# A decode block on Trainium2: the first weight load issued as two on the same queue, 16 partitions and then the other 112

## The chip, the cores and the metric

The kernel runs on one core of a Trainium2 chip. The metric is the time of one execution on the device in microseconds (us), as the median of several runs. Everything is float32. The five engines named below are TensorE (PE in the profile, with PEld for its loads of stationary operands), VectorE (DVE), ScalarE (ACT), GpSimd (POOL) and SyncE (SP). DMAs are issued from SP or from ACT, each of which has a queue of its own, and the DMA engines carry them out.

## What is computed

One decode step of a transformer block for eight sequences with one new token each: layer norm, attention over the last 1024 positions of a cache, then layer norm and a gated feed-forward layer, both with a residual.

```python
B, D = 8, 1024;  Hq, Hkv, Dh = 32, 4, 128;  Df = 3584
def _A_ref(x, k_cache, v_cache, wq, wo):
    W = min(4096, max(256, Sk // 4))                 # 1024
    q = (x @ wq).reshape(B, 1, Hq, Dh).transpose(0, 2, 1, 3)
    k = repeat(k_cache[:, :, Sk - W:, :], Hq // Hkv, axis=1)
    v = repeat(v_cache[:, :, Sk - W:, :], Hq // Hkv, axis=1)
    p = softmax(einsum("bhqd,bhkd->bhqk", q, k) * Dh ** -0.5)
    o = einsum("bhqk,bhkd->bhqd", p, v)
    return o.transpose(0, 2, 1, 3).reshape(B, 1, Hq * Dh) @ wo
def _B_ref(x, w_gate, w_up, w_down):
    return (gelu(x @ w_gate) * (x @ w_up)) @ w_down
h  = x + _A_ref(layernorm(x), k_cache, v_cache, wq, wo)
h2 = h + _B_ref(layernorm(h), w_gate, w_up, w_down)      # the result
```

## The kernel before

With eight rows of activations, nearly all the work is bringing weights and cache from HBM into SBUF. These are laid out on the host into twelve units of 128 partitions by 16,384 floats (65,536 bytes for each partition, 8.39 MB for each unit): two for wq, two for the keys, two for the values, two for wo, and four for gate and up, the last two of which carry some rows of w_down besides. What is left of w_down follows as four loads `dn`, three `tails` and two `ends`, which get smaller towards the end of the kernel.

There are two buffers in SBUF, `wbuf[0]` and `wbuf[1]`, each as large as one unit. Even units go to the first and odd units to the second. All weight loads are issued by `move` (line 91) on SP's queue in one order, in the loop of lines 150 to 155: units 0 and 1 without a wait, and unit u from 2 on after the matmuls that read unit u - 2. Those waits hold up SP, so all later loads stand behind them. In the first turn of that loop, x (eight rows of 4,096 bytes, into partitions 0, 4, ..., 28 of `x_sb`) is issued on ACT's queue, behind a memset of `x_sb` on GpSimd.

A load adds 16 to a semaphore when all of it has landed. Units count on `go[0]` or `go[1]`, one for each buffer. VectorE adds 1 more to it when the stationary operands of that unit (`still[0]` or `still[1]`) are ready, and TensorE's `half` (line 214) takes 17 from it before it begins its 64 matmuls on the buffer. So a half begins when both its weights and its activations are there.

The steps up to the first matmuls on weights are: x lands; `layernorm` (line 247) on VectorE, with one square root on ScalarE, writes `source`; TensorE transposes it in eight pieces into `turned` (line 240); `spread(0)` (line 271) copies `turned` with VectorE into `still[0]` and `still[1]`, one copy for each, each adding its 1 to `go`; then `half(0, ...)` reads unit 0 and, in the next turn of TensorE's loop, `half(1, ...)` reads unit 1. `spread` is called again at the second layer norm, as `spread(5)`.

`run` (line 80) gives an instruction the waits it is handed: `start` (line 71) leaves out those that the engine has already seen, issues all but the last as waits of their own, and puts the last on the instruction.

Of the kernel before, what the change touches and what calls it, by code (L numbers as in the profile page):

```python
# [7 lines left out]
P = 128  # L8
# [6 lines left out]
NC = D // P  # L15
NQ = 4
# [25 lines left out]
class Flow:  # L42
# [37 lines left out]
    def run(self, engine, make, *waits, mark=True, gives=None):  # L80
        ins = self.start(engine, make, waits)
        if gives is not None:
            ins.then_inc(*gives)
            return None
        if not mark:
            return None
        self.done[engine] += 1
        ins.then_inc(self.own[engine], 1)
        return self.own[engine], self.done[engine]

    def move(self, name, out, src, *waits, engine="sync", sem=None):
        s = self.sem(name) if sem is None else sem
        self.start(engine, lambda e: e.dma_start(out, src), waits).then_inc(s, 16)  # L93
        return s, 16


def decode_block(nc, x, units, dn, tails, ends, outs):

    fl = Flow(nc)
    run, move = fl.run, fl.move  # L100
# [10 lines left out]
    wbuf = [space[:, i * BUF:(i + 1) * BUF] for i in range(2)]  # L111
# [6 lines left out]
    go = [fl.sem("go_a"), fl.sem("go_b")]  # L118
# [4 lines left out]
    at_mark = {}  # L123
# [26 lines left out]
    for u in range(UNITS):  # L150
        k, i = divmod(u, 2)
        free = None if k == 0 else (half_a, half_b)[i](k - 1)
        move(f"u{u}", wbuf[i], units[u], free, sem=go[i])
        if u == 0:
            x_in = move("x", x_sb[0:ROWS:STEP, :], x, x_zero, engine="scalar")

# [19 lines left out]
    for i, (n, src) in enumerate(zip(ENDS, ends)):  # L176
        t = wbuf[1][:, c0:c0 + NQ * n]
# [69 lines left out]
    def layernorm(src, ready, name, room):  # L247

        bn = sb(name + "_bn", ROWS, D // N, 6)
        tok = None  # L250
        for i in range(D // N):
            tok = run("vector", lambda e, i=i: e.bn_stats(bn[:, i], src[:, i * N:(i + 1) * N]), ready)
        mv, ve, sd, r0, r1, r2, rs = (
            sb(f"{name}_{n}", ROWS, k) for n, k in
            (("mv", 2), ("ve", 1), ("sd", 1), ("r0", 1), ("r1", 1), ("r2", 1), ("rs", 1))
        )
        tok = run("vector", lambda e: e.bn_aggr(mv, bn), tok)
        tok = run("vector", lambda e: e.tensor_scalar(ve, mv[:, 1:2], EPS, None, op0=ALU.add), tok)
        tok = run("scalar", lambda e: e.activation(sd, ve, AF.Sqrt), tok)
        tok = run("vector", lambda e: e.reciprocal(r0, sd), tok)  # L260

        tok = run("vector", lambda e: e.scalar_tensor_tensor(
            r1, r0, r0, ve, op0=ALU.mult, op1=ALU.mult), tok)
        tok = run("vector", lambda e: e.tensor_scalar(
            r2, r1, -0.5, 1.5, op0=ALU.mult, op1=ALU.add), tok)
        tok = run("vector", lambda e: e.tensor_mul(rs, r0, r2), tok)
        run("vector", lambda e: e.tensor_scalar(
            source[0:ROWS], src, mv[:, 0:1], rs, op0=ALU.subtract, op1=ALU.mult), tok, room,
            gives=(go_turn, 1))

    def spread(k):

        for i in range(2):
            run("vector", lambda e: e.tensor_copy(  # L274
                still[i].rearrange("p (c j m) -> p c j m", c=NC, j=NQ),
                turned.rearrange("p (c m) -> p c m", c=NC)[:, :, 0:32].unsqueeze(2).to_broadcast(
                    [P, NC, NQ, 32])), at_mark["t", k], gives=(go[i], 1))


    layernorm(x_sb, x_in, "ln1", src_ok)  # L280
    spread(0)


    side_by_side = [source[:, hf * N:(hf + 1) * N] for hf in range(2)]
# [12 lines left out]
    for hf in range(2):  # L297
# [3 lines left out]
        for s in range(2):  # L301
            for a in range(2):
                for b in range(HB):
# [6 lines left out]
                        gives=(go[hf], 1) if end else None)  # L310
# [3 lines left out]
    for hf in range(2):  # L314
# [7 lines left out]
        if hf == 1:  # L322
            run("vector", lambda e: e.tensor_copy(still[0], turned), at_mark["t", 2], half_a(1),
                gives=(go[0], 1))
# [4 lines left out]
        gives=(go[1], 1))  # L329


    for hf in range(2):
# [3 lines left out]
        for h in range(2):  # L336
            o3 = sums[hf][:, h * N:(h + 1) * N].rearrange("p (b d) -> p b d", b=HB)
            for b in range(HB):
# [5 lines left out]
                else:  # L344
# [3 lines left out]
                        gives=(go_turn, 1) if end and hf else None)  # L348
        cleared[hf] = run("gpsimd", lambda e: e.memset(still[hf], 0.0), done(2))  # L349

    for hf in range(2):
# [12 lines left out]
        gives=(go_fold, 1))  # L364
    h_sb = sb("h_sb", ROWS, D)
    h_ok = run("vector", lambda e: e.tensor_add(h_sb, x_sb, turned[0:ROWS]), at_mark["y", 3])
    layernorm(h_sb, h_ok, "ln2", None)
    run("gpsimd", lambda e: e.memset(note[:, 7:8], 0.0), at_mark["t", 5], gives=(go_fold, 2))
    spread(5)
    rest = sb("rest", P, N)  # L370
    for ch in range(2):
# [8 lines left out]
    for k, n in enumerate(SETS):  # L380
# [5 lines left out]
        if k == 1:  # L386
# [9 lines left out]
            gives=(go_turn, 1))  # L396
        t = turned[:, 0:N].rearrange("p (i m) -> p i m", m=P)
# [9 lines left out]
        else:  # L407
# [3 lines left out]
                at_ok, gives=(go_later[0], 1))  # L411
# [5 lines left out]
    for ch in range(2):  # L417
        p0 = 32 * (2 + ch)
# [137 lines left out]
```

## Time and profile before

| | |
|---|---|
| median of three runs | 263.91 us (263.86 to 264.18) |
| the profiled execution's own time | 264.18 us |
| its span in the profile | 262.9 us |
| moved by DMA | 111.33 MB, mean 424 GB/s |
| busy: TensorE, VectorE, ScalarE, GpSimd | 54%, 17%, 5%, 3% of the span |
| mean granted TensorE clock | 0.79 |

The span reaches from the first to the last instruction that the profile shows of one execution; the time of that execution is 1.3 us longer. In the views below, a busy row gives microseconds of work with the number of instructions in brackets. "DMA share" is the mean busy share of the core's 16 DMA engines in a stretch, and "GB/s" what they moved; both count a packet with the stretch in which it begins, so in short stretches a share can be over 1. In a timeline a line gives the start and the length in us, the engine, the line of the kernel, the operation, the tiles and the number of instructions, and in brackets for how long the engine was idle before and what ended that.

### The profile page before, as it was taken

The numbers are of one execution on the slowest core, as the hardware profiler recorded it, in microseconds if no ns is written. First come the engines' busy times: TensorE is split into PE (matmuls) and PEld (weight loads), VectorE is DVE, ScalarE is ACT, GpSimd is POOL, SyncE is SP. The second block draws the span as 40 slices with busy tenths as digits, with TensorE's granted clock in tenths as the row PEclk, the third lists the DMA queues.
The fourth block names the chain that finished last, engine by engine and source line by source line (L and its number), as shares of the span: only waits on it lengthen the run. The fifth ranks groups of instructions, "written<-read, shape, count | busy, mean of one in ns | idle before, by whom it ended". The sixth has DMA issues, their size and how long they took to land. (4 is left out here: it accounts for less than half of the span.)

```text
span 262.9 us, 2262 instructions
## 1 busy us (share of the span) xinstructions
PE 141.5 (54%) x968; PEld 44.5 (17%) x968; DVE 43.8 (17%) x115; ACT 13.5 (5%) x19; POOL 7.2 (3%) x18
## 2 busy tenths in 40 slices
PE   0025706926807927608908409728509709319985
PEld 0021201211202312102302102122103202002321
DVE  0340200240100140400410100254100300100432
ACT  1000000000030010000000200000300000200000
POOL 5000100100000000100100000000000000000000
PEclk9999975985966965975976956965957957956999
DMA  8997997999799899979979997997997999799996
GB/s 319 484 459 339 479 479 339 459 479 479 319 479 479 349 449 479 479 319 479 479 329 469 479 469 329 479 479 319 479 479 319 479 479 479 319 479 399 400 421 239
DMA packets 3329, 111.33 MB, mean 424 GB/s; under 512 B 504, under 2 KB 760, under 8 KB 1280
## 3 DMA queue, kind: packets, MB, share of 16 engines
q1 hardware_dynamic: 3168, 111.23, 98.4%
q10 hardware_dynamic: 160, 0.08, 0.1%
q8 instruction: 1, 0.02, 0.0%
HBM read 111.18 MB, written 0.13 MB: 423 GB/s over the span
## 5 line engine op out<-in xcount | busy, mean ns | idle before, releaser
L222 PE MATMUL sum<-w,still 128*32 128x512 f32 x832 | 117.2, 726 | 96.3 <-PEq L209 96.3
L222 PEld LDWEIGHTS sum<-w,still 128*32 128x32 f32 x832 | 32.2, 130 | 177.1 <-issue 177.1
L240 PE MATMUL turned<-ident,source 128*128 128x128 f32 x64 | 11.0, 328 | 21.1 <-PEq L209 21.0
L240 PEld LDWEIGHTS turned<-ident,source 128*128 128x128 f32 x64 | 8.7, 167 | 26.4 <-issue 26.4
L235 PE MATMUL turned<-y_sb,add 128*32 128x512 f32 x24 | 11.3, 592 | 0.9 <-PEq L209 0.9
L318 DVE TENSOR_REDUCE nmax<-sum 128x1 f32<-128x1024 f32 x2 | 2.4, 1223 | 28.4 <-PE sum L222 28.4
L393 DVE TENSOR_TENSOR up<-up,sum 128x512 f32<-128x512 f32 (+1 forms) x2 | 1.4, 686 | 34.3 <-PE sum L222 34.3
L289 DVE TENSOR_SCALAR q<-sum 128x512 f32<-128x512 f32 x2 | 1.4, 692 | 25.2 <-PE sum L222 25.2
L274 DVE COPY still<-turned 128x1024 f32<-128x1024 f32 x4 | 4.7, 1219 | 4.2 <-PE turned L240 4.2
L383 DVE TENSOR_TENSOR gate<-gate,sum 128x512 f32<-128x512 f32 (+1 forms) x2 | 1.4, 685 | 23.6 <-PE sum L222 23.6
L345 DVE SCALAR_TENSOR_TENSOR o<-sum,share,o 128x128 f32<-128x128 f32 x12 | 4.2, 351 | 4.2 <-PE sum L222 3.8
L342 DVE TENSOR_SCALAR o<-sum,share 128x128 f32<-128x128 f32 x2 | 0.7, 350 | 24.0 <-PE sum L222 24.0
L320 ACT ACT_TABLE_LOAD x1 | 1.3, 1283 | 60.2 <-DVE nmax L318 60.2
L235 PEld LDWEIGHTS turned<-y_sb,add 128*32 128x32 f32 x24 | 2.6, 110 | 8.7 <-issue 8.7
L349 POOL MEMSET still<- 128x1024 f32 x2 | 1.9, 951 | 76.0 <-PE sum L222 76.0
L362 DVE TENSOR_TENSOR y_sb<-y_sb,sum 128x512 f32<-128x512 f32 x1 | 0.7, 686 | 15.8 <-PE sum L222 15.8
L294 POOL MEMSET still<- 128x1024 f32 x2 | 1.9, 957 | 46.5 <-PE sum L222 46.5
L360 ACT COPY y_sb<-sum 128x512 f32<-128x512 f32 x1 | 0.6, 586 | 50.7 <-PE sum L222 50.7
L320 ACT ACTIVATE source<-sum,nmax 128x1024 f32<-128x1024 f32 x2 | 2.2, 1113 | 17.1 <-PE turned L240 17.1
L361 DVE TENSOR_TENSOR y_sb<-y_sb,sum 128x512 f32<-128x512 f32 x1 | 0.7, 686 | 14.3 <-PE sum L222 14.3
L305 DVE COPY still<-turned 128x16 f32<-128x16 f32 x32 | 2.7, 161 | 2.1 <-PE turned L240 2.1
L382 ACT COPY gate<-sum 128x512 f32<-128x512 f32 (+1 forms) x2 | 1.2, 584 | 30.4 <-PE sum L222 30.4
(61 smaller groups left out, 40.3 us busy)
## 6 DMA issues: line engine op xcount, KB each, us to landing
w<-dn SPq DMA_DIRECT2D x1, 4096.0 KB, 19.8
w<-dn SPq DMA_DIRECT2D x1, 2048.0 KB, 24.3
w<-dn SPq DMA_DIRECT2D x2, 1024.0 KB, 27.3
w<-tails SPq DMA_DIRECT2D x3, 512.0 KB, 12.0
w<-ends SPq DMA_DIRECT2D x1, 320.0 KB, 13.1
w<-units SPq DMA_DIRECT2D x12, 29.4
w<-ends SPq DMA_DIRECT2D x1, 192.0 KB, 13.1
out<-o_fin SPq DMA_DIRECT2D x1, 80.0 KB, 1.6
```

Source lines behind the costliest of these rows:

```text
L222: ins = PE.matmul(sums[i][32 * j:32 * j + 32, h * N:(h + 1) * N], still[i][:, 32 * s:32 * s + 32], wbuf[i][:, s * N:(s + 1) * N], start=(c ...
L235: ins = PE.matmul(turned[0:32, ch * N:(ch + 1) * N], add2[:, ch, :], y_sb, start=True, stop=True)
L240: ins = PE.transpose(turned[:, n * P:(n + 1) * P], source[:, n * P:(n + 1) * P], ident)
L274: run("vector", lambda e: e.tensor_copy(still[i].rearrange("p (c j m) -> p c j m", c=NC, j=NQ), turned.rearrange("p (c m) -> p c m", c=NC) ...
L289: tok = run("vector", lambda e: e.tensor_scalar(q_sb, sums[hf][:, 0:N], scale, None, op0=ALU.mult), done(0, 0))
L294: cleared.append(run("gpsimd", lambda e: e.memset(still[hf], 0.0), done(0)))
L305: run("vector", lambda e: e.tensor_copy(to[:, :, b, s, a, REP * b:REP * b + REP].rearrange("p k (h i) -> p k h i", h=2), frm[:, s, a * HB ...
L318: tok = run("vector", lambda e: e.tensor_reduce(out=nmax, in_=sums[hf], axis=AX.X, op=ALU.max, negate=True), done(1))
L320: p_ok = run("scalar", lambda e: e.activation(source, sums[hf], AF.Exp, bias=nmax, accum_out=tot), tok, at_mark["t", 1 + hf])
L345: tok = run("vector", lambda e: e.scalar_tensor_tensor(out, o3[:, b], share[hf][:, b:b + 1], o_sb, op0=ALU.mult, op1=ALU.add), tok, done(2 ...
L349: cleared[hf] = run("gpsimd", lambda e: e.memset(still[hf], 0.0), done(2))
L383: tok = run("vector", lambda e: e.tensor_add(gate[:rows], gate[:rows], sums[0][:rows, N:2 * N]), tok, half_a(4 + k))
```

## The change

The load of unit 0 is issued as two loads, one behind the other on SP's queue. The first, `first`, brings rows 0 to 15 into partitions 0 to 15 of `wbuf[0]` and counts on a semaphore of its own. The second brings rows 16 to 127 into the other 112 partitions and counts on `go[0]`, as the whole unit did. The loads of the other eleven units run over partitions 0 to 127, as before. Since TensorE's wait on `go[0]` no longer covers the first 16 rows, `spread(0)`, which adds the 1 to `go[0]` and so releases the half, waits for `first` too.

```diff
     for u in range(UNITS):
         k, i = divmod(u, 2)
         free = None if k == 0 else (half_a, half_b)[i](k - 1)
-        move(f"u{u}", wbuf[i], units[u], free, sem=go[i])
+        p0 = 0
+        if u == 0:
+            p0 = 16
+            first = move("first", wbuf[i][0:p0], units[u][0:p0])
+        move(f"u{u}", wbuf[i][p0:P], units[u][p0:P], free, sem=go[i])
         if u == 0:
             x_in = move("x", x_sb[0:ROWS:STEP, :], x, x_zero, engine="scalar")
...
-    def spread(k):
+    def spread(k, *waits):
...
-                    [P, NC, NQ, 32])), at_mark["t", k], gives=(go[i], 1))
+                    [P, NC, NQ, 32])), at_mark["t", k], *waits, gives=(go[i], 1))
...
-    spread(0)
+    spread(0, first)
```

## The prediction

> **What bounds the kernel now.** I read the page first (the slices, the DMA queues, the chain that ended last), then busy time by 20 us stretches, then the first microseconds one by one, then the timeline of the first 32 us and the DMA issues of SP. From the page:
>
> ```profile
> span 262.9 us, 2262 instructions
> ...
> DMA  8997997999799899979979997997997999799996
> GB/s 319 484 459 339 479 479 339 459 479 479 319 479 479 349 449 479 479 319 479 479 329 469 479 469 329 479 479 319 479 479 319 479 479 479 319 479 399 400 421 239
> ...
> q1 hardware_dynamic: 3168, 111.23, 98.4%
> ...
> DMA 5%; PE 4%; SPq 0%; issue 0%; DVE 0%
> ```
>
> The line of q1 is the kernel. SP's queue carries 111.23 MB, and its packets fill 98.4% of what 16 DMA engines have in 262.9 us, 258.7 us of each. The chain that ended last accounts for a few per cent only, because it begins late, at the last buffer that was set free. What sets the time is that every DMA engine works through its sixteenth of the bytes without a pause. The dips in the GB/s row are no pauses: a packet's bytes are counted where it begins, so a slice holds two or three rounds of large packets. By stretches:
>
> ```profile
> core 0: us, PE busy (x) PEld busy (x) DVE busy (x) ACT busy (x) POOL busy (x), PEclk, DMA share, GB/s
> 20.00:40.00 20.00, 8.71 (x64) 2.38 (x64) 1.38 (x2) 0.00 (x0) 0.96 (x1) 0.91 0.97 419
> 40.00:60.00 20.00, 11.98 (x76) 3.88 (x76) 4.07 (x34) 0.00 (x0) 0.96 (x1) 0.76 0.97 419
> 60.00:80.00 20.00, 9.83 (x64) 2.65 (x64) 1.62 (x3) 2.49 (x3) 0.00 (x0) 0.67 1.02 442
> 200.00:220.00 20.00, 11.89 (x84) 3.77 (x80) 2.57 (x5) 0.58 (x1) 0.00 (x0) 0.76 0.97 419
> ```
>
> The last two columns matter. A share of 0.97 at 419 GB/s is one load of 8.39 MB (128 partitions of 65,536 bytes) in 19.4 us of each engine; shares over 1 come from the same counting by beginnings. TensorE is busy for about half of each stretch at any granted clock. There is no idle DMA time in which a delay of the queue could be made up later. So a delay of the slowest DMA engine in the first load goes to the end in full, and a gain there too. Now the first microseconds, with the same columns:
>
> ```profile
> 0.00:1.00 1.00, 0.00 (x0) 0.00 (x0) 0.00 (x0) 0.00 (x0) 0.47 (x5) 1.00 0.00 0
> 1.00:2.00 1.00, 0.00 (x0) 0.00 (x0) 0.00 (x0) 0.00 (x0) 0.93 (x3) 1.00 1.93 655
> 2.00:3.00 1.00, 0.00 (x0) 0.00 (x0) 0.28 (x1) 0.06 (x1) 1.00 (x3) 1.00 1.03 393
> 3.00:4.00 1.00, 0.00 (x0) 0.00 (x0) 0.00 (x0) 1.00 (x1) 0.92 (x5) 1.00 0.00 0
> 4.00:5.00 1.00, 0.00 (x0) 0.00 (x0) 0.00 (x0) 0.23 (x1) 0.00 (x0) 1.00 1.51 655
> 5.00:6.00 1.00, 0.00 (x0) 0.00 (x0) 0.00 (x0) 0.00 (x0) 0.00 (x0) 1.00 0.91 393
> ```
>
> 655 and 393 GB/s over 1 us are 0.655 and 0.393 MB, that is 10 and 6 packets of 65,536 bytes: a round of 16, one row of one partition for each DMA engine. The first round begins between 1 and 3 us and takes 1.93 + 1.03 = 2.96 us of each engine; the second begins between 4 and 6 us and takes 1.51 + 0.91 = 2.42 us. So a round of 16 rows costs 2.42 us once the queue runs, eight rounds are the 19.4 us of above, and the first round loses 0.54 us.
>
> **The change part by part.** It replaces one load of 128 rows (eight rounds) by one of 16 rows (one row for each engine) and one of 112 (seven for each, 7 x 16 = 112), on the same queue, adds one DMA issue on SP, one semaphore, and one wait on DVE ahead of the first spread. The rows that carry these parts, first from the timeline, then from the groups of issues (shortest, median and longest ns, first and last start):
>
> ```profile
> 1.70 1.21 ACTq L93 DMA_DIRECT2D x_sb<-x  x1
> ...
> 10.47 1.28 DVE L252 BATCH_NORM_STATS2 ln_bn<-x_sb 32x6 f32<-32x512 f32 x2 [7.97 <-DMA x_sb<-x]
> ...
> 16.21 2.35 DVE L274 COPY still<-turned 128x1024 f32<-128x1024 f32 x2 [2.12 <-PE turned L240]
> ...
> 22.68 8.71 PE L222 MATMUL sum<-w,still 128*32 128x512 f32 x64 [6.51 <-PEq L209]
> ```
>
> ```profile
> L93 SPq DMA_DIRECT2D w<-units x12: 328/328/425, 0.7 to 205.8; - x12
> L93 SPq DMA_DIRECT2D w<-tails x3: 327/432/432, 245.6 to 246.4; - x3
> ```
>
> ```profile
> 31.45 0.33 SPq L93 DMA_DIRECT2D w<-units  x1
> ```
>
> The extra issue: 0.33 to 0.43 us of SP. The 16 rows are issued at 0.7 us as u0 is now, the 112 rows 0.4 us behind them, and u1 0.4 us later than now. All of this lies under the first round, which ends after 4 us; cost 0. Uncovered it would be 0.43 us.
>
> The wait on DVE: the spread at 16.21 us waits for the transposes and now also for the 16 rows. Behind it on DVE stand the second spread and then the work on the first sums, which needs the matmuls at 22.68 us; those need the spread and all of u0. The spreads end at 18.56 us, 4.1 us before the matmuls begin, so one semaphore wait more (I allow 0.1 us) costs 0. Even where the 16 rows come late, the 112 rows stand behind them on the same queue, and the matmuls wait for those longer. Cost 0.
>
> x travels on ACT's queue, lands at about 10.4 us, and the chain from there to the end of the spreads is 8.1 us. If the first round grows, x may land later by as much; so does u0 in that case, and the 4.1 us stay. Cost 0.
>
> u2 is issued at 31.45 us, when the matmuls of u0 are over, and u1 by then still has some 10 us to run (it begins on the engines when u0 ends, near 22 us, and takes 19.4 us). If u0 lands late, u1 ends late by as much on the slowest engine, so this cover holds where it matters. An engine that is ahead may run dry there; it is not the one that ends last.
>
> The rows themselves are the unknown. In the old load the 16 engines write into 128 partitions, eight for each; the first of the new ones makes all 16 write into 16 neighbouring partitions at once. Every weight load of this trace fills all 128 partitions, so whether the 2.42 us of a round is set by the DMA engines or by the partitions written into isn't shown. x, with 8 rows, only shows waiting. Bounds: if the engines set it, the 16 rows take a round, 2.42 us, and the 112 rows seven rounds, 16.9 us: no loss. If the partitions set it, an eighth of the partitions takes the bytes at an eighth of the rate: 8 x 2.42 = 19.4 us for the 16 rows, a loss of 17.0. For the 112 rows the engines would each hold seven neighbouring rows. A grouping that gives each of 16 engines a part of SBUF for itself when there are eight rows for each no longer does so with seven, and two engines meet in one part. If they do at every row, the 112 rows take 14 rounds, 33.9 us, another loss of 16.9. The loss lies between 0 and 33.9 us. Both halves of it have the same sign and size, and no row leans to one end of it, so I take the middle, 16.9 us.
>
> [...]
>
> The start has a gain to offer: an engine that is handed one row instead of eight may begin sooner. The first round's excess of 0.54 us is the most that I can find for it; the same start later by the same amount bounds it on the other side. I take 0.
>
> Sum against the profiled execution: 264.18 us (its span of 262.9 us and 1.3 us around it) plus 16.9 is 281.1; the median of the three runs, 263.91, lies 0.27 us lower, so the forecast is 280.8 us.
>
> **The rivals.** First: the engines set the pace and the start is gained. For it: each engine's packets stand end to end, at 419 GB/s in stretch after stretch, as they would with engines that are simply full. Against it: the gain is 0.54 us at most, and comes only if 16 engines writing into 16 partitions are as fast as into 128. Gain and no gain give 263.4 and 263.9 us; it decides for a faster kernel only from a gain of 0.53 us, which is 0.2%, about what a measurement of this kernel can tell from no change. So this case is split: 0.06 faster, 0.10 the same, 0.01 slower by a worse start. Chance 0.17.
>
> Second: only the 16 rows lose, and the 112 rows run as fast as seven rounds of now. For it: seven of eight rounds keep 16 engines spread over 112 partitions. Its middle loss is half of 17.0, 8.5 us: 272.4 us. Chance 0.15.
>
> Third: the 112 rows are dealt out so that several engines meet in one place at each row, as in the 16 rows. From the top of the bounds, 33.9 us, it gives 297.8 us, and more if more than two meet. Against it: seven rows in a block for each engine is the plain way to divide 112. Chance 0.10, of which 0.03 above 298.
>
> That the change does nothing (the split is made and everything lands as before) is the 0.10 of the first.
>
> **How the numbers follow.** The forecast case, both loads lose something near the middle, has what is left, 0.58; its own range is 275 to 288 us. What carries it is the asymmetry of the bounds: everything except the lowest end of them is a loss of many us, the gain is capped at 0.54, and the queue's share of 98.4% leaves nowhere to hide either. The range leaves out the first rival (0.17) and the top of the third (0.03): it reaches from 269 us, under the second rival, to 298 us. Faster 0.06, the same 0.10, slower 0.58 + 0.15 + 0.10 + 0.01 = 0.84.
>
> **What would show it.** In the changed profile the stretches of 1 us should have the first 16 packets with a summed share well over 2.96 us (near 11 by the middle of 2.42 and 19.4), nothing beginning behind them until they end, x landing later than 10.4 us, and the first matmuls of line 222 some 17 us after 22.68. From about 60 us on every stretch should read 0.97 and 419 GB/s again, with all later work moved by the same amount, and the share of q1 in the longer span should stay high on account of packets that take longer, not of more bytes. Wrong would be: the second round beginning between 4 and 6 us as now (the first rival); matmuls only 7 to 9 us late (the second); over 30 us late (the third); or a delay of u0 that is gone at the end, which would mean that the queue had slack after all.

## The result and the profile after

The changed kernel takes 285.8 us (median of six runs, 285.65 to 287.35) against 264.03 us before in the same comparison: a ratio of 1.0836, 95% interval 1.0824 to 1.0849, or 21.8 us more. The forecast was 16.9 us more, at 280.8 us, in a range from 269 to 298 us.

The page of the profile after, the same lines as of before:

```profile
span 284.3 us, 2264 instructions
...
DMA  9799799999999999999999999998999999989994
GB/s 148 148 300 277 166 277 424 443 433 424 396 415 433 433 433 443 443 443 443 443 443 443 433 433 443 415 424 387 433 433 433 443 443 443 443 383 438 410 411 167
...
q1 hardware_dynamic: 3184, 111.23, 98.0%
...
DMA 5%; PE 4%; SPq 0%; DVE 0%; issue 0%
```

The busy row of DMA says 7 or 9 in the first six slices and 9 nearly everywhere behind them, much as it did before, yet the GB/s row says 148 to 300 in those six. The queue holds the same 111.23 MB, and 16 more packets; by the packet records (the trace's list of every packet with its start, its length and its bytes) these have 4 bytes each, and there are 16 of that size for each issue on SP's queue: 352 for 22 issues before, 368 for 23 now. The engines are as busy as before (98.0% against 98.4%) over a longer span (284.3 us against 262.9). So the time went into packets that take longer, not into waiting. By stretches of 20 us the loss has a place:

```profile
0.00:20.00 20.00, 0.00 (x0) 0.00 (x0) 0.29 (x1) 1.28 (x1) 3.32 (x13) 1.00 0.95 159
20.00:40.00 20.00, 1.94 (x8) 1.57 (x8) 5.42 (x11) 0.20 (x1) 0.00 (x0) 1.00 1.02 262
40.00:60.00 20.00, 9.73 (x64) 2.64 (x64) 1.38 (x2) 0.00 (x0) 0.96 (x1) 0.92 1.00 413
60.00:80.00 20.00, 11.32 (x76) 3.66 (x76) 4.07 (x34) 0.00 (x0) 0.96 (x1) 0.76 0.97 419
```

The last two columns: a share near 1 with 159 and 262 GB/s for 40 us, then 419 again. From here on the two profiles run alike, one behind the other. The timeline shows the delay of unit 0 (the window asked for ends at 52 us, so the last row counts 44 of the 64 matmuls):

```profile
21.90 1.27 DVE L256 BATCH_NORM_STATS2 ln_bn<-x_sb 32x6 f32<-32x512 f32 x2 [19.40 <-DMA x_sb<-x]
...
27.70 2.36 DVE L278 COPY still<-turned 128x1024 f32<-128x1024 f32 x2 [2.19 <-PE turned L244]
...
44.63 7.58 PE L226 MATMUL sum<-w,still 128*32 128x512 f32 x44 [17.03 <-PEq L213]
```

The matmuls of unit 0 begin at 44.63 us in place of 22.68, 21.95 us later; the span is 21.4 us longer. x came 11.4 us later and the spreads with it, but they end at 30.06 us and the matmuls still wait 14.6 us for the weights.

The rounds of the first load can be read one by one. A window that holds the beginnings of all 16 packets of a round, and of no others, has share times length = mean packet time (and GB/s times length = 1.05 MB where there are 16). First the 16 rows, then the seven rounds of the 112 (the second of these rows counts six short packets of x too), then the first round of unit 1:

```profile
1.00:3.00 2.00, 0.00 (x0) 0.00 (x0) 0.29 (x1) 0.06 (x1) 1.93 (x5) 1.00 4.22 524
9.00:11.50 2.50, 0.00 (x0) 0.00 (x0) 0.00 (x0) 0.00 (x0) 0.00 (x0) 1.00 2.24 419
15.70:16.60 0.90, 0.00 (x0) 0.00 (x0) 0.00 (x0) 0.00 (x0) 0.00 (x0) 1.00 5.43 1192
20.40:21.40 1.00, 0.00 (x0) 0.00 (x0) 0.00 (x0) 0.00 (x0) 0.00 (x0) 1.00 3.10 1049
23.50:25.90 2.40, 0.24 (x1) 0.27 (x2) 1.53 (x6) 0.20 (x1) 0.00 (x0) 1.00 1.53 437
27.10:29.50 2.40, 0.50 (x3) 0.10 (x1) 1.79 (x2) 0.00 (x0) 0.00 (x0) 1.00 1.86 437
31.20:34.10 2.90, 0.00 (x0) 0.00 (x0) 0.00 (x0) 0.00 (x0) 0.00 (x0) 1.00 1.60 362
35.90:38.70 2.80, 0.00 (x0) 0.00 (x0) 0.00 (x0) 0.00 (x0) 0.00 (x0) 1.00 1.61 374
40.40:43.50 3.10, 0.00 (x0) 0.00 (x0) 0.00 (x0) 0.00 (x0) 0.00 (x0) 1.00 1.07 338
```

The 16 rows take 2.00 x 4.22 = 8.44 us each, against 2.96 before. The 112 rows take 5.60, 4.9 (4.8 without x's packets), 3.10, 3.67, 4.46, 4.64 and 4.51 us, together 30.9 us, against seven times 2.42, 16.9. The first round of unit 1 still takes 3.32 us while the last engines are at work on unit 0; after it the pace is 2.42 again. So the mean engine loses 5.5 + 13.9 + 0.9 = 20.3 us, and the engine that is last 1.5 us more: in the packet records the ends of the round of unit 1 that follows lie 2.2 us apart where they lay 0.4 apart before, and the last of them is 1.7 us behind the mean where it was 0.2.

### The profile page after: what moved, and what is told of

Same layout as the page of the kernel before. It is cut to its first block, busy times and chain, and to the rows that moved or that the text cites. A ratio compares the mean times of both kernels' runs of the same rounds, so it can differ in the third digit from the quotient of the medians.

```text
span 284.3 us, 2264 instructions
## 1 busy us (share of the span) xinstructions
PE 140.5 (49%) x968; PEld 43.4 (15%) x968; DVE 43.8 (15%) x115; ACT 13.5 (5%) x19; POOL 7.2 (3%) x18
## 3 DMA queue, kind: packets, MB, share of 16 engines
q1 hardware_dynamic: 3184, 111.23, 98.0%
## 5 line engine op out<-in xcount | busy, mean ns | idle before, releaser
L244 PE MATMUL turned<-ident,source 128*128 128x128 f32 x64 | 10.0, 306 | 32.5 <-PEq L213 32.5
L244 PEld LDWEIGHTS turned<-ident,source 128*128 128x128 f32 x64 | 7.9, 155 | 37.8 <-issue 37.8
L387 DVE TENSOR_TENSOR gate<-gate,sum 128x512 f32<-128x512 f32 (+1 forms) x2 | 1.4, 686 | 21.8 <-PE sum L226 21.8
L256 DVE BATCH_NORM_STATS2 ln_bn<-x_sb 32x6 f32<-32x512 f32 x2 | 1.3, 672 | 19.4 <-DMA x_sb<-x 19.4
## 6 DMA issues: line engine op xcount, KB each, us to landing
w<-dn SPq DMA_DIRECT2D x1, 4096.0 KB, 20.3
```

The lines of the kernel that those rows point to most:

```text
L244: ins = PE.transpose(turned[:, n * P:(n + 1) * P], source[:, n * P:(n + 1) * P], ident)
L387: tok = run("vector", lambda e: e.tensor_add(gate[:rows], gate[:rows], sums[0][:rows, N:2 * N]), tok, half_a(4 + k))
```

## The experiments

Theory S says that the loss comes from the SBUF side: a load that gives the 16 DMA engines rows in too few parts of SBUF at a time is slow (a part is a group of partitions that would share one way in; that there are such parts is the author's supposition; no run shows them, or which partitions each would hold). The rivals were that a second load on the queue, its semaphore or the added wait cost the time (Q), or the order of rows in HBM (H), or that the 112 rows suffered only from standing behind the 16 (W). Later came theory C, that engines that meet in one part slow all the others to their own pace, and its rival N, that they slow only themselves. Single runs are compared with the 264.0 to 264.1 us of before on the same chip; the six runs of the changed kernel spread over 1.7 us, so smaller differences between single runs show nothing. Unless another kernel is named, an edit is made to the changed kernel; `...` stands for lines left out.

**The same two loads, split by columns.**

`SET` is 2,048 of the 16,384 columns, an eighth.

```diff
-        p0 = 0
+        n0 = 0
         if u == 0:
-            p0 = 16
-            first = move("first", wbuf[i][0:p0], units[u][0:p0])
-        move(f"u{u}", wbuf[i][p0:P], units[u][p0:P], free, sem=go[i])
+            n0 = SET
+            first = move("first", wbuf[i][:, 0:n0], units[u][:, 0:n0])
+        move(f"u{u}", wbuf[i][:, n0:BUF], units[u][:, n0:BUF], free, sem=go[i])
```

> Unit 0 is still brought by two loads on SP's queue with the same share of bytes (an eighth, then seven eighths) and the same extra wait on DVE, but split by columns, so that each of the two fills all 128 partitions. Theory S (SBUF side: a load pays for writing into too few partitions at once): no loss, 263.4 to 264.4 us, matmuls of unit 0 begin within 0.6 us of the 22.7 us of before. Rival Q (the second load on the queue, its semaphore or the DVE wait cost the time): slower as in the change, near 285.8 us. Rival H (HBM side: rows that are read at the same time lie badly in HBM): no loss either.

Measured: 263.88 us against 264.06, ratio 0.9995, interval 0.9986 to 1.0004. The timeline has the matmuls of unit 0 in their old place:

```profile
22.52 9.48 PE L226 MATMUL sum<-w,still 128*32 128x512 f32 x64 [7.35 <-PEq L213]
```

Two loads, one more issue, one more semaphore and one more wait cost nothing that can be measured. Q is out: only the cut across partitions costs.

**Rows that lie further apart in HBM.** `u0` is unit 0 in an array of its own, its rows padded by 1,024 floats.

```diff
...
+        src = units[u]
         if u == 0:
             p0 = 16
-            first = move("first", wbuf[i][0:p0], units[u][0:p0])
-        move(f"u{u}", wbuf[i][p0:P], units[u][p0:P], free, sem=go[i])
+            src = u0[:, 0:BUF]
+            first = move("first", wbuf[i][0:p0], src[0:p0])
+        move(f"u{u}", wbuf[i][p0:P], src[p0:P], free, sem=go[i])
...
```

> The change as it is, with unit 0 read from an array of its own in HBM whose rows lie 69,632 bytes apart instead of 65,536. Theory S: nothing changes, 285 to 287 us, the first 16 packets again take about 8.5 us each. Rival H: the packets get faster, the first 16 towards 2.4 to 3 us, and the time falls towards 264 us. Rival Q: 285 to 287 us.

Measured: 285.81 us. The first 16 packets take 2.00 x 4.23 = 8.46 us:

```profile
1.00:3.00 2.00, 0.00 (x0) 0.00 (x0) 0.28 (x1) 0.06 (x1) 1.93 (x5) 1.00 4.23 524
```

The pitch of the rows in HBM changes nothing, which speaks against H. The narrow extra load and its control, further down, speak against it too: both read one contiguous block of the same size and differ in the partitions that they fill, and so in the length of their packets (28,672 and 3,584 bytes).

**112 rows first, then 16.**

```diff
-            p0 = 16
+            p0 = P - 16
...
```

(`first` is then the load of partitions 0 to 111, and the other 16 follow; the other units are loaded whole, as before.)

> Unit 0 as 112 rows first (partitions 0 to 111) and the 16 rows of partitions 112 to 127 behind them. Theory S: the cost belongs to each load by itself and the order does not matter: about +20 us (282 to 288 us); the first seven packets of each engine already take 3.5 to 5 us, the eighth about 8 us. Rival theory W: the 112 rows were slow only because the 16 rows ahead of them had put the engines out of step; then the 112 rows run at 2.4 us a packet and only the 16 rows cost, about +6 us, 270 us.

Measured: 285.32 us. The second round of the 112 rows and the round of the 16 rows, now the eighth:

```profile
5.20:6.80 1.60, 0.00 (x0) 0.00 (x0) 0.00 (x0) 0.00 (x0) 0.00 (x0) 1.00 2.98 655
30.90:35.60 4.70, 0.00 (x0) 0.00 (x0) 0.00 (x0) 0.00 (x0) 0.00 (x0) 1.00 1.76 223
```

They are 1.60 x 2.98 = 4.77 us and 4.70 x 1.76 = 8.27 us. W is out: each load is slow wherever it stands.

**Two halves of 64 partitions.**

```diff
-            p0 = 16
+            p0 = 64
```

> Unit 0 as two loads of 64 partitions, 0 to 63 and 64 to 127. Theory S, with a rate that goes with how many parts of SBUF a load reaches: every packet takes 1.75 to 2 times 2.42 us, 4.2 to 4.8 us, for all eight rounds, so +14.5 to +19.3 us, 278 to 283.5 us. If only very narrow loads suffered: below 270 us. Rival Q: near 285.8 us, as any two loads.

Measured: 285.75 us, above the range that was expected for it. The rounds are even, 4.8 us in the first and 4.9 to 5.2 in the others; these two take 1.10 x 4.66 = 5.13 us, 2.12 times 2.42 and not 1.75 to 2 times:

```profile
27.00:28.10 1.10, 0.00 (x0) 0.00 (x0) 0.23 (x1) 0.00 (x0) 0.00 (x0) 1.00 4.66 953
32.10:33.20 1.10, 0.00 (x0) 0.00 (x0) 0.00 (x0) 0.00 (x0) 0.00 (x0) 1.00 4.66 953
```

That the time equals the change's is chance: here the eight rounds cost 2.6 us more each on the mean, there one costs 5.5 and seven cost 2.0 each.

**Sixteen-row loads whose partitions are known.**

```diff
...
-            p0 = 16
-            first = move("first", wbuf[i][0:p0], units[u][0:p0])
-        move(f"u{u}", wbuf[i][p0:P], units[u][p0:P], free, sem=go[i])
+            firsts = [move(f"s{o}", wbuf[i][o:112:7], units[u][o:112:7]) for o in range(7)]
+            move(f"u{u}", wbuf[i][112:P], units[u][112:P], sem=go[i])
+        else:
+            move(f"u{u}", wbuf[i], units[u], free, sem=go[i])
...
-    spread(0, first)
+    spread(0, *firsts)
```

> Unit 0 as seven loads of 16 rows, each into every seventh partition (o, o + 7, ..., o + 105), and the last 16 rows into partitions 112 to 127; each load has a semaphore of its own that the spread waits for. Every load now gives each DMA engine exactly one row, so which partitions are written at the same time is known. Theory C (coupling: when two of the 16 engines write into the same part of SBUF, all 16 fall to the pace of those two): all 16 packets of a spaced load take 3 to 5 us, and the time is that of the run with 112 rows first, 285 us within 1.5 us. Rival theory N (only the engines that meet are slowed, by a factor of two): at most 4 of the 16 packets of each load take 4.8 us, the others 2.4 us, and the time is 270 to 278 us.

Measured: 285.81 us. The second, third, fourth and eighth of the loads:

```profile
5.80:7.60 1.80, 0.00 (x0) 0.00 (x0) 0.00 (x0) 0.00 (x0) 0.00 (x0) 1.00 2.66 583
10.50:12.40 1.90, 0.00 (x0) 0.00 (x0) 0.00 (x0) 0.00 (x0) 0.00 (x0) 1.00 2.65 569
15.40:17.40 2.00, 0.00 (x0) 0.01 (x1) 1.45 (x5) 0.18 (x1) 0.00 (x0) 1.00 1.75 524
31.30:35.00 3.70, 0.00 (x0) 0.00 (x0) 0.00 (x0) 0.00 (x0) 0.00 (x0) 1.00 2.28 283
```

By share times length these are 4.79, 5.04 (4.85 without x's packets, which this window counts too), 3.50 and 8.44 us. The time is the one that theory C expected and is far above the 270 to 278 us of N. In the packet records all 16 packets of the second load take 4.74 to 4.95 us, none 2.42. The seven spaced loads, with one row for each engine, take 4.1, 4.8, 4.8, 3.5, 3.5, 4.5 and 4.9 us; the seven rounds of the run with 112 rows first take 4.0, 4.8, 4.8, 3.2, 3.7, 4.7 and 4.9, which fits a division of the 112 rows into blocks of seven (all by the weights' packets alone).

Which rows meet, and so how many packets N would have slow, was supposed; no run shows it. What the packet records do show is that rounds differ: in the third of the seven rounds of the changed kernel two packets stand at 4.62 and 4.65 us and the other fourteen at 2.75 to 3.10; in its second all 16 stand at 4.74 to 4.88.

**The 112 rows alone.** Partitions 0 to 15 of unit 0 are zeroed by GpSimd in place of the first load, so of each 128 rows of wq's first half the first 16 count as zero.

```diff
-            first = move("first", wbuf[i][0:p0], units[u][0:p0])
+            first = run("gpsimd", lambda e: e.memset(wbuf[0][0:16], 0.0))
```

> The load of the 16 rows is left out: partitions 0 to 15 of unit 0 are zeroed by GpSimd, so a sixteenth part of the second half of the work is not what the reference computes there (16 of the first 1024 rows of wq's product are missing). It prices the 112 rows alone. Theory S with coupling: the seven rounds take about 30 to 33 us where eight rounds of before took 20.2, so +10 to +13.5 us, 274 to 277.5 us. If the 112 rows were slow only behind the 16: seven rounds of 2.42, 261.6 us.

Measured: 275.52 us, 11.5 more than before with one round less to bring. The last of the seven rounds takes 2.90 x 1.57 = 4.55 us:

```profile
26.00:28.90 2.90, 0.00 (x0) 0.00 (x0) 0.00 (x0) 0.00 (x0) 0.00 (x0) 1.00 1.57 362
```

The 112 rows by themselves cost 11.5 + 2.42 = 13.9 us of the time over seven rounds of the old pace. That this is also the figure of the changed kernel's rounds is in part chance: the time includes the spread of the engines, the sum of the rounds does not. By the packet records the seven rounds take 29.8 us here, 12.3 more than the first seven of before (2.96 + 6 x 2.42 = 17.5; all eight are 19.9, not the 20.2 of the expectation); in the changed kernel they cost 13.9. The difference lies in the first round of the 112 rows, which there begins while other engines are still at work on the 16.

**The narrow load alone, and its control.** Both are made to the kernel before; the control has `spare` of 896 floats and fills all 128 partitions of it with the same number of bytes.

```diff
...
+    spare = sb("spare", P, 7168)
+    move("probe", spare[0:16], extra)
     for u in range(UNITS):
...
```

> The kernel before with one more load ahead of unit 0: 16 rows of 28,672 bytes into partitions 0 to 15 of a spare tile that nobody reads. It prices the narrow load alone. At the full pace of an engine its packets take 28,672 / 65,536 x 2.42 = 1.06 us, at the pace of the first 16 packets of the changed kernel 28,672 / 65,536 x 8.5 = 3.7 us. Theory S: +3.7 us within 0.6, 267.8 us. If the narrow load only cost together with the 112 rows behind it: +1.06 us, 265.1 us.

> The control to the extra load of 16 rows: the kernel before with one more load of the same 458,752 bytes ahead of unit 0, this one into 128 partitions of the spare tile, 3,584 bytes each. Theory S: it costs its bytes at the queue's pace, 1.06 us, 264.9 to 265.4 us, against the 267.7 us of the 16 rows. Rival: any extra load at the start costs about 3.7 us, 267.7 us.

Measured: 267.72 us into 16 partitions (ratio 1.0155, interval 1.0133 to 1.0177) and 264.96 us into 128 (1.0038, 1.0025 to 1.0051). The same bytes cost 2.76 us more in 16 partitions; scaled from 28,672 to 65,536 bytes a row that is 6.3 us, near the 5.5 us of the changed kernel's first round. The wide one costs 0.93 us, about its bytes (1.06). Both times are as expected, but the 16 packets of the narrow load do not take the 3.7 us that the expectation gave them:

```profile
1.70:2.50 0.80, 0.00 (x0) 0.00 (x0) 0.29 (x1) 0.00 (x0) 0.72 (x3) 1.00 3.70 573
```

They take 0.80 x 3.70 = 2.96 us, 2.8 times 1.06. The rest of the loss is in the round behind them, whose packets take 3.2 to 4.5 us in the packet records where the first round of before had 2.5 to 3.3.

**The change made to unit 1.**

```diff
-        if u == 0:
+        if u == 1:
             p0 = 16
...
-                    [P, NC, NQ, 32])), at_mark["t", k], *waits, gives=(go[i], 1))
+                    [P, NC, NQ, 32])), at_mark["t", k], *(waits if i else ()), gives=(go[i], 1))
```

> The change made to unit 1 in place of unit 0 (16 partitions of the second buffer, then the other 112; the second spread waits for the 16 rows). Theory S with no slack in the queue: the loss belongs to the narrow loads wherever they stand, +20 to +22 us, 284 to 286 us, and unit 0 runs at 2.42 us a packet as before. Rival theory T (a good part of the loss is the start of the queue, cold and out of step): clearly less, below 280 us.

Measured: 287.01 us, 23.0 more than before and 1 us above what was expected (a single run; those of the changed kernel reach 287.35). The 16 rows, now issued into a running queue, take 1.10 x 7.92 = 8.7 us:

```profile
21.60:22.70 1.10, 0.00 (x0) 0.00 (x0) 0.00 (x0) 0.00 (x0) 0.00 (x0) 1.00 7.92 953
```

So the loss is not one of the start, and the queue has no slack in the second load either.

**Two rows into partitions 126 and 127.** The kernel before, with two rows of 28,672 bytes into those partitions of a spare tile between units 0 and 1; the load of unit 2 also waits for them.

```diff
...
+        if u == 1:
+            probe = move("probe", spare[126:P], extra)
-        move(f"u{u}", wbuf[i], units[u], free, sem=go[i])
+        move(f"u{u}", wbuf[i], units[u], free, probe if u == 2 else None, sem=go[i])
...
```

> The kernel before with one more load between units 0 and 1: two rows of 28,672 bytes into partitions 126 and 127 of a spare tile, so that two DMA engines write where one engine of unit 1 writes as well, and nothing else collides. Theory C (coupling): while that lasts, packets of all 16 engines take clearly more than 2.42 us (3 us or more in one round). Rival N: about three engines show packets of 3 to 5 us and the other thirteen keep 2.42 us. The time, 265 to 267.5 us, is about the same in both.

Measured: 267.04 us, in the range that was expected. The round before the two rows, and the one in which they fall:

```profile
19.30:19.90 0.60, 0.00 (x0) 0.00 (x0) 0.00 (x0) 0.00 (x0) 0.00 (x0) 1.00 4.03 1748
21.80:22.30 0.50, 0.00 (x0) 0.00 (x0) 0.00 (x0) 0.00 (x0) 0.00 (x0) 1.00 5.64 1950
```

The mean goes from 0.60 x 4.03 = 2.42 to 0.50 x 5.64 = 2.82 us (with two short packets in it). In the packet records three packets are hit: one of unit 1 takes 4.63 us, and the two short ones 2.2 and 2.4 us where 2.42 us scaled by their bytes is 1.06. The other thirteen take 2.69 to 2.80 us. That these three write into one part is not shown, only that three are hit, as many as the expectation has there. This is neither C nor N as they stood: all are slowed, but the thirteen only by 11 to 16% and not to the pace of the three. C in its strong form falls here. The changed kernel's third round looks alike, with two packets at 4.62 and 4.65 us and the others at 2.75 to 3.10.

**32 and 96 partitions.**

```diff
-            p0 = 16
+            p0 = 32
```

> The change with 32 partitions and then 96. By theory C with the parts of SBUF that the runs so far fit, the 32 rows meet in pairs everywhere (5.1 us a packet, as in the two halves), and each of the six rounds of the 96 rows has at least two meeting pairs (4.7 us): 2 x 5.1 + 6 x 4.7 = 38.4 us against 19.4, +19 us and up to 3 us more for the last engine, 283 to 286.5 us. If the loss went with how narrow the first load is, it would be about half of the change's: 275 us.

Measured: 284.36 us, 20.3 more than before and in the range of the first expectation. The second round of the 32 rows takes 1.60 x 3.21 = 5.14 us, the second of the 96 rows 1.30 x 3.93 = 5.11:

```profile
6.00:7.60 1.60, 0.00 (x0) 0.00 (x0) 0.00 (x0) 0.00 (x0) 0.00 (x0) 1.00 3.21 655
16.30:17.60 1.30, 0.04 (x1) 0.07 (x2) 0.96 (x3) 0.00 (x0) 0.00 (x0) 1.00 3.93 807
```

A first load that is twice as wide does not halve the loss, since both parts of the cut are slow. The pairs that meet in the expectation were supposed; the run shows the length of the packets alone.

**A smaller first part by columns.** As the first experiment, with `n0 = N` (512 columns).

> The split by columns with a smaller first part: 128 partitions by 2,048 bytes, then the rest. If engines begin sooner when the first load is short, the first round's excess of 0.54 us is partly won: 263.5 to 263.9 us. If nothing at the start is to be had: 264.0 us within 0.3.

Measured: 264.06 us against 264.03, ratio 1.0001, interval 0.9992 to 1.0010. There is no gain at the start to be had in this way. No version here beats the kernel before.

## Why the prediction was right, and where its sizes were off

**The bound.** That the queue has no idle time, so that a delay in the first load goes to the end in full, held: 21.95 us at the first matmuls, 21.4 us at the end of the span, and the same for a later load (unit 1, 23.0 us in the time).

**The costs put at nothing.** The extra issue, the semaphore, the wait on DVE, x's later landing and u2's later issue were priced at 0; the split by columns keeps the issue, the semaphore and the wait, and costs nothing. u2's later issue is covered as the prediction says: it is issued at 54.42 us, and in the packet records the engines are at work on u1 until 61 to 63 us. x came 11.4 us later, and not by the 5.5 that the first round grew, since it lands when the third round ends (20.5 to 21.2 us), and three rounds grew. That still cost nothing: the 4.1 us between the spreads and the matmuls did not stay but became 14.6.

**The 16 rows.** The prediction's bounds were 2.42 and 19.4 us, its middle a loss of 8.5. Measured were 8.44 us a packet, a loss of 5.5 in the changed kernel and 6.3 scaled from the extra load. They take 3.5 times as long as at the full pace, where the upper bound had eight times.

**The 112 rows.** This is the term that was mis-sized. The middle of its bounds was a loss of 8.5 us; measured were 13.9 in the rounds of the changed kernel; the 112 rows alone cost 12.3 by their rounds and 13.9 by the time. The prediction's upper bound, two engines meeting at every row and 14 rounds, 33.9 us, was close (30.9), though that two engines meet was a supposition that no run shows. It took the middle because no row of before leaned to one end, as if meetings came at about half of the rows. The runs show instead that a load of 16 spaced rows can have all 16 packets at 4.7 to 5.0 us, and that most rounds are slow: of the changed kernel's seven, five take 4.5 to 5.6 us and two take 3.1 and 3.7. The two errors, 3.0 us too much and 5.4 too little, partly cancel and bring 16.9 to 19.3. That the forecast came within about 5 us of the measured time is in part luck, since both middles were choices between far bounds and not read from a row. The rest, up to the 21.8 us of the times, is the spread of the engines, which the prediction gave no price: 0.9 us in the first round of unit 1, and 1.5 us by which the last engine then lags further behind the mean than before.

**The rivals.** No loss with a better start: refuted by the change itself, and the splits by columns show that even without the loss there is no gain of 0.5 us. Only the 16 rows lose: refuted by the 112 rows alone. The third, the 112 rows dealt so that several engines meet in one place as in the 16, has the time too high (297.8); no round of the 112 is as slow as the 8.4 us of the 16, and blocks of seven, which the prediction held against it, are what fits. The rows named ahead as signs moved as the forecast case said, though not by its sizes: first matmuls 22 us late where 17 was named, packets of the first round 8.4 us where about 11 was named.

**What stays open.** Why all 16 packets run at half pace in some rounds (4.74 to 4.88 us in the changed kernel's second of the 112 rows), while 13 of them lose only 11 to 16% beside the two extra rows and fourteen lose 14 to 28% in the changed kernel's third. One other reading, that an engine is slow because it writes into a part that is another engine's in the wide loads, was not tested. That the loss lies in the partitions written is shown: the split by columns costs nothing, and the same bytes cost 2.76 us more in 16 partitions than in 128. That engines meet in parts of SBUF is the author's explanation, not shown by a run, and the blocks of seven are inferred from the agreement with the order of the rounds.

## What to carry to other kernels

In a kernel whose DMA queue is never idle, cut a load by columns and leave all 128 partitions in each part: here that cost nothing (263.88 us against 264.06), while a cut across partitions made one load of 8.39 MB take 41.6 us in place of 20.4, from the start of its first packet to the end of its last, and 64 + 64 was no better than 16 + 112 (285.75 and 285.8 us). Look at the share and the GB/s rows together: here a share near 1 at 159 GB/s meant slow packets, and an earlier issue would have found no idle time to use. And when a term's bounds lie far apart, ask whether its events average out or whether the slowest sets the pace of all; here the second was nearer: in five of the seven rounds of the 112 rows every packet took over 4 us.

## What the runs showed of the hardware that was not expected

Rows into half of the partitions ran at less than half the pace: 5.13 us a packet in the halves of 64, 2.12 times 2.42. Rows into an eighth of them, partitions 0 to 15, ran at more than an eighth of it: 8.44 us a packet, 3.5 times 2.42. And two rows into partitions 126 and 127 during the load of unit 1 slowed thirteen other packets of that round a little too, from 2.42 to about 2.75 us.
